# A searched table of due times, whole feature products on GpSimd, and MLP blocks of four tiles in a two-layer attention and MLP kernel

## The chip, the cores and the metric

The kernel runs on one core of one Trainium2 chip. The metric is the device time of one execution in microseconds (us). The profile's span (first to last instruction) is about 1.8 us shorter than that time, so spans are compared with spans and times with times. PE is the matmul engine, DVE the vector engine, ACT the scalar engine, POOL is GpSimd, and SP issues most DMAs.

## The reference, cut to what matters

```python
for layer in range(2):                      # the same weights in both layers
    n = layernorm(x)                        # 2048 tokens of 512, in 16 tiles of 128
    q, k, v = split(n @ wqkv)               # 32 heads of 16
    phi = lambda u: concat(softmax(u @ w_phi), softmax(-(u @ w_phi)))   # 32 features a head
    kv, z = phi(k).T @ v, phi(k).sum()      # over ALL tokens: a barrier in each layer
    x = x + (phi(q) @ kv / (phi(q) @ z + 1e-6)) @ wo
    n = layernorm(x)
    x = x + (relu(n @ W_gate) * (n @ W_up)) @ W_down        # 512 -> 1376 -> 512
```

The sum over all tokens splits each layer: first the keys of all 16 tiles, then attention and MLP tile by tile. The keys of layer 1 are made tile by tile as the MLP of layer 0 ends.

## The kernel before: the parts that matter

Each instruction group is an `Op` with an engine, an estimated cost (time the engine is held, time to the result), what it waits for, and a *due time*. A list scheduler inside the kernel, `plan`, runs all of them on paper and fixes the order on each engine. Only that order goes into the program. `port=True` marks DVE and POOL instructions which the planner keeps from overlapping on paper.

```python
for e, cand in open_.items():               # in plan(): each engine's ready operations
    ...
    t = max(clock[e], o.ready, port if o.port else 0.0, lanes[0] if o.move else 0.0)
    ...                                     # of those that can start first, the least due time wins
def refine(ops, rounds):                    # due times: plan forward, plan backward, ten times
    ...
XPOSE = (1200, 2430)                        # a DMA transpose: 1.2 us to issue, 2.43 us to land
RATE = 265.0
BLOCKS = ((1, 1, 2, 2, 2, 2, 2, 2, 2), (1, 1, 2, 2, 2, 2, 2, 2, 1, 1))   # MLP tiles per block
```

Layer 0, per tile: statistics, the scaling `xn` (DVE), a transpose (`xnTA`), K and V products (PE), two exponentials `ek` (ACT), a sum `sk` (DVE), its reciprocal (ACT), the feature product `phiK`, then the accumulating product `kvz` (PE):

```python
        n = op("DVE", SCALE, due, lambda: nc.vector.tensor_scalar(          # xn
            out=xn.t[:], in0=x_of(t), scalar1=mv[:, t, 0:1], scalar2=rs[:, t:t + 1], ...), port=True)
        ...
        a = [op("DVE", dve(512), ..., phi(nc.vector, 0, 1), ..., port=True),    # "BOTH": half on DVE
             op("POOL", (965, 975), ..., phi(nc.gpsimd, 1, 1), ..., port=True)] # half on POOL
```

In attention each tile's result `o` is transposed by DMA on SP (`oT`), and a PE projection with `wo` follows. The MLP does the same with its own input (`xnTB`). The transposes are issued one after another on SP; in the trace of the kernel before one takes 1.2 us to issue and 2.4 us to land in the median of the layers, 3.0 in the first stage.

The softmax here doesn't subtract the row's maximum and nothing guards it: scores larger than these inputs give would overflow.

## Time and profile before

| | before |
|---|---|
| time, median of the first 3 runs | 402.7 us (402.51 to 403.94) |
| span of the profiled run | 401.2 us |
| PE time by matmul count and spacing | 379.8 us |
| start of the last kvz of layer 0 | 60.4 us |
| sum of PE holes to the last matmul | 15.2 us |
| last matmul start to end of span | 3.9 us |

The third row is the number of matmuls of each width times their back-to-back spacing in the trace (216 ns for 512 columns, 109 for 256, 56 for 128). A hole is what is left between two matmul starts after that spacing.

The page of the kernel before, busy shares and the busy tenths of 40 equal slices:

```profile
PE 387.8 (97%) x3176; PEld 265.9 (66%) x3176; DVE 275.5 (69%) x685; ACT 259.5 (65%) x704; POOL 22.1 (6%) x24
...
PE   6889999899999999999999999999999999999996
...
DVE  6999896999995835787365457799998523132222
...
POOL 0142350000000000000000002000000000000000
```

PE is almost always busy, so only its holes can be won. They lie in the first six slices (60 us) and in a few later ones. The view of stretches of the kernel before (stretch, its length, busy us of each engine with instruction counts, clock, DMA share, GB/s) shows who fills the first 60 us:

```profile
10.00:20.00 10.00, 8.38 (x52) 4.16 (x53) 10.00 (x23) 8.52 (x28) 1.93 (x2) 1.00 0.23 63
20.00:30.00 10.00, 8.40 (x84) 5.32 (x81) 9.88 (x14) 8.02 (x24) 4.86 (x5) 1.00 0.82 190
30.00:40.00 10.00, 9.28 (x57) 4.55 (x56) 9.93 (x23) 8.66 (x28) 2.23 (x2) 1.00 0.73 162
40.00:50.00 10.00, 9.72 (x57) 4.95 (x58) 8.88 (x16) 9.51 (x30) 3.06 (x4) 1.00 0.93 263
50.00:60.00 10.00, 10.00 (x84) 6.05 (x82) 9.45 (x10) 9.64 (x27) 5.96 (x6) 1.00 0.42 120
```

The third busy figure is DVE: 8.9 to 10 us of every 10. Feature products and xn scalings of the kernel before in that time (views by tile; min/median/max in ns, first and last start in us):

```profile
L466 POOL TENSOR_TENSOR phiK<-ek,sk x16: 1054/1056/1717, 16.5 to 58.9; 128x512 bf16<-128x512 bf16 x16
L466 DVE TENSOR_TENSOR phiK<-ek,sk x16: 652/692/1358, 17.9 to 58.8; 128x512 bf16<-128x512 bf16 x16
L427 DVE TENSOR_SCALAR xn<-X,mvA,rsA x15: 390/403/1097, 11.5 to 45.8; 128x512 bf16<-128x512 bf16 x15
```

This is the waits view of the kernel before from 62 us to the end, PE alone (who waited for whom: us, times, longest):

```profile
PE b L607 <- ACT Eq L522: 0.4, 2, 0.3
PE b L565 <- DVE X L569: 0.4, 1, 0.4
PE q L536 <- ACT N L543: 0.4, 1, 0.4
PE b L565 <- ACT oT L376: 0.3, 1, 0.3
PE b L446 <- DMA xnTA<-xn: 0.3, 1, 0.3
```

No wait for a DMA transpose of `oT` is in it, though 28 of the 32 projections take their input from one.

### The profile page before, as it was taken

What the parts mean: (1) busy time and instruction counts of PE and PEld (TensorE: products, weight loads), DVE (VectorE), ACT (ScalarE), POOL (GpSimd) and SP (SyncE); (2) the same over time, 40 slices, a digit from 0 to 9 for tenths busy, and PEclk for the clock granted to TensorE, in tenths of its full rate; (3) what the DMA queues carried; (4) which work ended last, traced back from release to release, by engine and by line L of the source; (5) the groups of instructions that cost most, each with busy time, mean ns of one, the idle gap of its engine ahead of it and who ended that gap; (6) DMA issues with size and microseconds to landing.
All of it is one profiled execution on the core that took longest, in us unless ns stands there. A gap on an engine that the chain in (4) does not pass through costs nothing.

```text
span 401.2 us, 8365 instructions
## 1 busy us (share of the span) xinstructions
PE 387.8 (97%) x3176; PEld 265.9 (66%) x3176; DVE 275.5 (69%) x685; ACT 259.5 (65%) x704; POOL 22.1 (6%) x24
## 2 busy tenths in 40 slices
PE   6889999899999999999999999999999999999996
PEld 3454565667787678556777845576778686785784
DVE  6999896999995835787365457799998523132222
ACT  4888999977665355838464759997846353452542
POOL 0142350000000000000000002000000000000000
PEclk9999999999999999999999999999999999999999
DMA  6287940233331013101010100025333102001000
GB/s 211 63 192 159 262 118 0 42 67 63 71 68 41 0 28 67 26 15 28 2 26 2 28 0 2 1 41 81 68 65 68 28 26 68 13 29 39 15 28 28
DMA packets 54536, 21.83 MB, mean 54 GB/s; under 512 B 45952, under 2 KB 53472, under 8 KB 54496
## 3 DMA queue, kind: packets, MB, share of 16 engines
q1 hardware_dynamic: 53424, 20.25, 22.4%
q10 hardware_dynamic: 1072, 1.05, 0.8%
q8 instruction: 25, 0.41, 0.4%
q14 instruction: 15, 0.12, 0.1%
HBM read 8.44 MB, written 2.10 MB: 26 GB/s over the span
## 4 chain that ended last, share of the span: by engine, by line
PE 76%; DVE 14%; DMA 4%; ACT 3%; issue 2%; DVEq 0%; ACTq 0%
PE b L607 35%; PE b L642 18%; PE b L452 5%; PE b L446 5%; PE b L565 4%; PE b L518 3%; PE q L481 3%; DMA xnTA<-xn 3%; DVE pr L558 2%; ACT Eq L522 1%; DVE bstA L416 1%; PE q L536 1%; DVE X L569 1%; DVE m L553 1%; DVE o L561 1%
## 5 line engine op out<-in xcount | busy, mean ns | idle before, releaser
L619 ACT ACTIVATE gu<-b 128x512 bf16<-128x512 f32 (+1 forms) x102 | 55.5, 555 | 61.0 <-PE b L607 60.1
L607 PE MATMUL b<-xnTB,wg 128*128 128x256 bf16 (+3 forms) x836 | 92.9, 256 | 0.4 <-ACT Eq L522 0.3
L607 PE MATMUL b<-xnTB,wu 128*128 128x256 bf16 (+3 forms) x836 | 92.9, 256 | 0.2 <-ACT Eq L522 0.2
L625 DVE TENSOR_TENSOR hT<-gu 128x512 bf16<-128x512 bf16 (+1 forms) x102 | 38.5, 380 | 69.2 <-ACT gu L622 69.0
L642 PE MATMUL b<-wd,hT 128*128 128x512 bf16 (+1 forms) x352 | 82.8, 379 | 0.0
L607 PEld LDWEIGHTS <-wg 128*128 128x128 bf16 (+1 forms) x836 | 72.5, 100 | 11.4 <-issue 0.6
L607 PEld LDWEIGHTS <-wu 128*128 128x128 bf16 (+1 forms) x836 | 72.4, 100 | 8.1 <-issue 0.3
L622 ACT CAST gu<-b 128x512 bf16<-128x512 f32 (+1 forms) x102 | 54.8, 543 | 24.7 <-PE b L607 23.4
L642 PEld LDWEIGHTS <-hT 128*128 128x128 bf16 (+1 forms) x352 | 33.8, 98 | 34.8
L543 ACT CAST N<-q 128x384 bf16<-128x384 f32 (+1 forms) x96 | 48.1, 583 | 0.0
L522 ACT ACTIVATE Eq<-b 128x512 bf16<-128x512 f32 x64 | 40.4, 690 | 5.7 <-PE b L518 5.7
L457 DVE TENSOR_REDUCE sk<-ek 128x64 f32<-128x1024 bf16 x32 | 38.6, 1211 | 6.8 <-ACT ek L449 6.7
L648 DVE SCALAR_TENSOR_TENSOR X<-b,rsB,X 128x512 bf16<-128x512 f32 x32 | 23.3, 745 | 27.5 <-PE b L642 27.4
L449 ACT ACTIVATE ek<-b 128x512 bf16<-128x512 f32 x64 | 35.7, 603 | 8.9 <-PE b L446 8.6
L446 PE MATMUL b<-Wk,xnTA 128*128 128x512 bf16 x128 | 32.3, 380 | 4.2 <-DMA xnTA<-xn 2.1
L466 POOL TENSOR_TENSOR phiK<-ek,sk 128x512 bf16<-128x512 bf16 x18 | 21.4, 1193 | 226.6 <-ACT sk L462 221.9
L565 PE MATMUL b<-wo,oT 128*128 128x512 bf16 x128 | 32.5, 379 | 1.1 <-DVE X L569 0.4
L466 DVE TENSOR_TENSOR phiK<-ek,sk 128x512 bf16<-128x512 bf16 (+1 forms) x32 | 31.2, 977 | 2.4 <-ACT sk L462 2.3
L452 PE MATMUL b<-wv,xnTA 128*128 128x512 bf16 x128 | 32.2, 379 | 0.0
L518 PE MATMUL b<-xnTA,Wq 128*128 128x512 bf16 x128 | 31.7, 379 | 0.0
L543 ACT COPY DS<-q 128x48 f32<-128x48 f32 (+1 forms) x96 | 23.7, 318 | 7.2 <-PE q L536 6.1
L536 PE MATMUL q<-R,Eq 128*128 128x144 bf16 x256 | 25.1, 226 | 0.5 <-ACT N L543 0.4
(65 smaller groups left out, 376.1 us busy)
## 6 DMA issues: line engine op xcount, KB each, us to landing
out_dram<-X SPq DMA_DIRECT2D x16, 128.0 KB, 1.7
X<-in_A_x_dram SPq DMA_DIRECT2D x6, 256.0 KB, 4.0
wg<-in_B_W_gate_dram SPq DMA_DIRECT2D x4, 344.0 KB, 3.8
wu<-in_B_W_up_dram SPq DMA_DIRECT2D x4, 344.0 KB, 3.8
wd<-in_B_W_down_dram SPq DMA_DIRECT2D x5, 256.0 KB, 3.1
wk<-in_A_wqkv_dram ACTq DMA_DIRECT2D x2, 256.0 KB, 3.6
X<-in_A_x_dram SPq DMA_DIRECT2D x4, 128.0 KB, 4.4
wv<-in_A_wqkv_dram ACTq DMA_DIRECT2D x1, 512.0 KB, 5.4
```

Source lines behind the costliest of these rows:

```text
L446: k = op("PE", mm(4, 512), due, lambda: [nc.tensor.matmul(kp.t[:], lhsT=xnTA[c][:, b, cols], rhs=Wk2[:, b, :], start=(b == 0), stop=(b == ...
L452: v = op("PE", mm(4, 512), due_v, lambda: [nc.tensor.matmul(vp.t[:], lhsT=xnTA[c][:, b, cols], rhs=wv[:, b, :], start=(b == 0), stop=(b == ...
L457: a = op("DVE", SUM16, due, lambda: nc.vector.tensor_reduce(out=sk.t[:], in_=ek.t[:].rearrange("p s (h f) -> p (s h) f", f=DH), axis=AX.X, ...
L466: e.tensor_tensor(out=ph.t[:, s:s + n].rearrange("p s (h f) -> p (s h) f", f=DH), in0=ek.t[:, s:s + n].rearrange("p s (h f) -> p (s h) f", ...
L518: q = op("PE", mm(4, 512), due(c, b), lambda b=b, qp=qp: [nc.tensor.matmul(qp.t[:], lhsT=Wq2[:, m, b * P:(b + 1) * P], rhs=xnTA[c][:, m, : ...
L522: done.append(op("ACT", act(512), due(c, b), lambda b=b, s=s, qp=qp: nc.scalar.activation(out=Eq[c][:, b, s, :], in_=qp.t[:], func=AF.Exp, ...
L543: nc.scalar.copy(out=q[:, k, 0:3] if k < 2 else q[:, :, 3], in_=ps.t[:, 0:n * GE].rearrange("p (n c j) -> p n c j", n=n, j=HB)[:, :, lo:hi])
L565: a = op("PE", mm(4, 512), due + 3, lambda: [nc.tensor.matmul(yp.t[:], lhsT=oT.t[:, b, :], rhs=wo[:, b, :], start=(b == 0), stop=(b == NB ...
L607: nc.tensor.matmul(ps.t[:m, q * W:(q + 1) * W], lhsT=w[:, b, g * P:g * P + m], rhs=xT.t[:, b, 0:W], start=(b == 0), stop=(b == NB - 1))
L619: nc.scalar.activation(out=gu.t[:m, 0, lo * W:hi * W], in_=gp.t[:m, lo * W:hi * W], func=AF.Relu)
L622: nc.scalar.copy(out=gu.t[:m, 1, lo * W:hi * W], in_=up.t[:m, lo * W:hi * W])
L642: nc.tensor.matmul(yp.t[:], lhsT=h.t[:m, f * W + i * P:f * W + (i + 1) * P], rhs=wd[:m, f, :], start=(f == 0), stop=(f == NF - 1))
```

## The change

The intent: feed the first stage faster (value weights loaded in two pieces, early tiles and query weights first, one late load between two transposes), take the feature products of layer 0 off the full DVE, use wider matmuls in the MLP (blocks of four tiles), shorten the tail (last product in two halves), and set the order by a table of due times, found by search, in place of the kernel's own refinement.

```diff
-def refine(ops, rounds):
+def arrange(ops):
+    assert len(ops) == len(DUE)
...
-        o.n = n
+        o.n, o.due = n, DUE[n]            # DUE: a table of 2080 searched numbers (cut)
...
-XPOSE = (1200, 2430)
-RATE = 265.0
+XPOSE, XPOSE_LOADS = (1200, 2430), (1200, 3500)
+RATE = 320.0
+PHI = ["POOL"] * 15 + ["BOTH"]
-BLOCKS = ((1, 1, 2, 2, 2, 2, 2, 2, 2), (1, 1, 2, 2, 2, 2, 2, 2, 1, 1))
+BLOCKS = ((1, 1, 2, 4, 4, 2, 2), (1, 1, 2, 4, 4, 2, 1, 1))
...
-    p_xB = pool("xnTB", 3, [NB, 2 * P], fifo=True)
-    p_h = pool("hT", 2, [NF * 2 * P], fifo=True)
+    p_xB = pool("xnTB", 2, [NB, 4 * P], fifo=True)
+    p_h = pool("hT", 2, [NF * 4 * P], fifo=True)      # wk, wq and their turned copy now live in hT
...
-    l_wv = [load(3, wv[:], wqkv[:, :, 2 * D:3 * D], 524288, "ACT")   (shortened)
+    l_wv = [load(0, wv[:, b:b + 2, :], ..., 262144, "ACT") for b in (0, 2)]
+    l_wq = [load(15 + b, wq[:, b, :], wqkv[:, b, 0:D], 131072) for b in range(NB)]   # was a late load
...
+            halves = ((0, 256), (256, 512)) if l == 1 and t == T - 1 else ((0, 512),)
...
-        keys.tile(t, k0, k0 + p["V0"], k0 + p["Z0"], xT[t], "BOTH")
+        keys.tile(t, k0, k0 + p["V0"], k0 + p["Z0"], xT[t], PHI[t])
```

## The prediction

> **What bounds the kernel now.** The busy table has PE at 387.8 of 401.2 us. Busy overlaps, so I summed the spacing of matmul starts in the trace: back to back, a 512-column matmul takes 216 ns, 256 columns 109, 128 columns 56; all 3176 come to about 380 us of streaming. PE idles about 15 us plus a 4 us tail. By stretch: 4.8 us (0 to 10), 1.7, 2.3, 1.2 (to 40), none to 60, 2.9 (60 to 100), 2.3 (250 to 270), else nothing. With the first weights landing at 5.0 us (chain of waits) and a tail of 3.5, a kernel without holes would take about 387 us.
>
> The early holes come from DVE: in the table of stretches it is 89 to 100% busy from 10 to 60 us, and the chain there alternates between DVE groups and transposes. Two transposes take 4.13 us against a median of 2.5[...] (DMA share 0.7 to 0.9 there).
>
> **What the change does.**
> 1. Keys of layer 0: the whole feature product goes to POOL for 15 of 16 tiles. DVE loses 15 halves of 789 ns, 12 us of its 54. POOL gets 15 x 2 x 1.05 us (uncontended half, timeline), 32 us, up to 36 at the mean of 1.19. [...]an xn scaling of 0.40 us takes 1.10 under a POOL product. POOL becomes a serial chain from about 18 to 55-57 us. The last kvz, now at 60.4, should come 3 us earlier.
> 2. Loads: early x tiles and query weights first, one late load instead of two between transposes. The instruction order shows key weights still issued before value weights, so "value weights first" does little, and the query fold now precedes the first K. I expect the first 12 us no better, transposes near 3 us, and 1.2 us of holes gone beyond item 1.
> 3. Blocks of four: 88 gate and up matmuls of 512 columns replace 176 of 256 in each of four blocks (216 against 2 x 109 ns): 0.8 us in all.
> 4. Last product in halves: the final add (0.75 us) halves, the store (128 KB, 1.7 us) shrinks a little: 0.4 us.
> 5. Searched due times fill part of the 5 us of holes at the two attention starts, which ScalarE bounds (19.5 of 20 us busy from 60 to 80): 1.5 us.
>
> Sum 6.9 us, nearly all on the chain, because it is PE idle time.
>
> **Predicted:** 395.8 us, 8 in 10 between 391 and 400.5. Faster by over 2% (under 394.6) 0.40, within 2% 0.57, slower 0.03.
>
> **What would show it.** Last kvz at 56 to 58 us; DVE's 18 half products down to about 3, POOL busy 35 to 40 us in the first 60; DVE no longer full there; xn scaling above its 426 ns mean; first-stage transposes near 3 us; no PE hole above 0.3 us after 100 us outside the second attention start; 341 fewer matmuls at nearly the same streaming sum, 379 us; the end 0.4 us shorter.
>
> **What would make it wrong.** POOL and DVE locking each other out more than planned, holding the last kvz at 60 us; the query fold delaying the first K; a block of four making PE wait for four tiles of attention between 70 and 110 us; or the search having removed nearly all holes (389 to 391).

The sum: 3 + 1.2 + 0.8 + 0.4 + 1.5 = 6.9 us, which takes 402.7 to 395.8. What the trace of the kernel before shows of DVE beside POOL: the xn scaling at 28.39 us took 1.10 us instead of 0.40 while two POOL products ran from 26.68 to 29.33, and the POOL product at 35.43 us took 1.72 us instead of 1.05 while a DVE product of 0.68 us ran.

## More of the kernel before

Runs at full clock lie mostly within 1 us of their median, but in some executions the granted TensorE clock is halved for a few microseconds near the start (0.50 from 12 to 16 us in the profile of e4), which costs about 2 us (beside e1 to e4 the kernel before took 404.1 to 404.8 us in its four runs with a mean clock of 0.996, and 401.7 to 402.7 in the other seven). The profile lists the mean clock of each run.

## The result, and the profile after

The changed kernel took 404.52 us (median of 4 runs, 404.31 to 405.02); the kernel before in the same session took 403.12 us. Ratios here are the mean time of one kernel's fast runs over that of the other's of the same rounds, so not quite the ratio of the medians: 1.0035, 95% interval 1.0012 to 1.0058. Its verdict is "same" at 2%, but the sign is against the prediction, and the time lies outside the predicted range. A second session (e5 below) gave 1.0074.

| profiled runs, both at full clock | before | after | difference |
|---|---|---|---|
| span | 401.2 | 402.6 | +1.4 |
| start of the last kvz of layer 0 | 60.4 | 61.1 | +0.7 |
| from the last matmul of that kvz to the last matmul of all | 336.5 | 337.8 | +1.3 |
| last matmul start to end of span | 3.9 | 3.3 | -0.5 |
| PE time by count and spacing | 379.8 | 379.1 | -0.7 |
| PE holes, 0 to 20 us | 6.5 | 4.9 | -1.6 |
| PE holes, 20 to 40 us | 3.5 | 2.9 | -0.5 |
| PE holes, 40 to 60 us | 0.0 | 2.1 | +2.1 |
| PE holes, 60 us to the end | 5.2 | 7.9 | +2.7 |

The holes that vanish before 40 us come back between 40 and 60, and new ones appear in the layers. The page of the changed kernel:

```profile
PE 387.8 (96%) x2835; PEld 231.8 (58%) x2835; DVE 269.5 (67%) x659; ACT 260.8 (65%) x696; POOL 34.3 (9%) x24
...
PE   7998989998999999999999999999999999999996
...
DVE  6989955999999828752584476599999423442232
...
POOL 0338680000000000000000003000000000000000
```

The stretches of the changed kernel. DVE is still 86 to 97% busy from 20 to 50 us and has room only from 50 to 60; POOL works up to 8.2 us in 10:

```profile
20.00:30.00 10.00, 9.29 (x55) 4.37 (x53) 8.64 (x16) 8.21 (x25) 3.07 (x3) 1.00 0.63 168
30.00:40.00 10.00, 8.37 (x56) 4.33 (x55) 9.15 (x16) 9.35 (x31) 8.23 (x5) 1.00 0.92 219
40.00:50.00 10.00, 9.69 (x75) 5.33 (x73) 9.67 (x12) 8.02 (x24) 6.93 (x4) 1.00 0.66 173
50.00:60.00 10.00, 8.83 (x63) 4.54 (x61) 5.92 (x6) 9.01 (x25) 8.21 (x5) 1.00 0.62 182
```

The same products and scalings in the changed kernel:

```profile
L571 POOL TENSOR_TENSOR phiK<-ek,sk x16: 1512/1928/1975, 15.7 to 59.4; 128x1024 bf16<-128x1024 bf16 x15, 128x512 bf16<-128x512 bf16 x1
L571 DVE TENSOR_TENSOR phiK<-ek,sk x1: 694/694/694, 59.3 to 59.3; 128x512 bf16<-128x512 bf16 x1
L531 DVE TENSOR_SCALAR xn<-X,mvA,rsA x14: 383/406/2146, 12.5 to 47.3; 128x512 bf16<-128x512 bf16 x14
```

A whole product takes 1.93 us on POOL. The longest xn scaling rose from 1.10 to over 2 us. All 16 xn scalings of layer 0 together took 7.1 us before and 12.4 after (summed from the trace); four of them took 1.4 to 2.1 us each. How that travels is seen in the timeline of the changed kernel from 45 us (start, us, engine and line, what, in brackets the idle time before and what ended it):

```profile
45.30 3.86 POOL L571 TENSOR_TENSOR phiK<-ek,sk 128x1024 bf16<-128x1024 bf16 x2 [1.35 <-PE q L586]
45.93 3.38 DVE L531 TENSOR_SCALAR xn<-X,mvA,rsA 128x512 bf16<-128x512 bf16 x2
...
49.23 2.33 DVE L562 TENSOR_REDUCE sk<-ek 128x64 f32<-128x1024 bf16 x2
...
51.49 3.81 POOL L571 TENSOR_TENSOR phiK<-ek,sk 128x1024 bf16<-128x1024 bf16 x2 [2.33 <-ACT sk L567]
...
53.48 0.64 PE L586 MATMUL q<-vext,phiK 128*128 128x129 bf16 x8 [0.78 <-POOL phiK L571]
```

Two POOL products run from 45.30 to 49.16. The two xn scalings that meet them end at 49.31 instead of after some 0.8 us. The sums `sk` behind them on DVE start only then. POOL then has nothing to do for 2.33 us, because its next product needs such a sum, and PE waits for POOL. So here two POOL products of 1.93 us each made the two scalings end some 2.6 us late, and the late sums left POOL idle for 2.33 us. In the waits view of the first 62 us, PE's longest wait in total is now for these products; the view of the kernel before lists no such wait of PE:

```profile
PE q L586 <- POOL phiK L571: 2.7, 5, 1.0
```

In the layers the waits view of the changed kernel (62 us to the end, PE) has a new first line:

```profile
PE b L670 <- DMA oT<-o: 2.4, 3, 1.3
PE b L670 <- ACT oT L480: 0.5, 1, 0.5
PE b L713 <- ACT xnTB L480: 0.5, 1, 0.5
PE q L641 <- ACT DS L648: 0.3, 1, 0.3
```

The three waits end near 98.5, 124.4 and 297.4 us. This is the first of them in the timeline of the changed kernel, SP's transposes and the projection:

```profile
93.89 1.20 SPq L508 DMA_TRANSPOSE xnTB<-xn  x1
95.20 2.06 SPq L508 DMA_TRANSPOSE oT<-o  x1
...
98.55 0.82 PE L670 MATMUL b<-wo,oT 128*128 128x512 bf16 x3 [1.25 <-DMA oT<-o]
```

This transpose held SP for 2.06 us instead of 1.2, and its projection came 3.35 us after its issue. The kernel before has a slow one at the same point of the layer, for the same tile:

```profile
93.59 2.37 SPq L404 DMA_TRANSPOSE oT<-o  x1
...
103.41 0.81 PE L565 MATMUL b<-wo,oT 128*128 128x512 bf16 x3
```

There PE only asks for the result 9.8 us later, so the slow transpose costs nothing. Over all 28 `oT` transposes on SP, the projection starts a median of 6.15 us after the transpose's issue in the trace of before (1 of 28 under 4 us), and 3.56 us in the changed kernel (20 of 28 under 4 us). The searched order has used up that slack.

The planner says how it came to that. Run on paper, `plan` gives the kernel before 396.5 us and the changed one 391.9. The search found 4.6 us in the plan, and the chip returned 1.4 us of loss. The measured span exceeds the plan by 4.7 us before and 10.7 us after. About half of that growth lies in the first stage: the plan starts the last kvz at 57.9 us before and 55.7 after, the chip at 60.4 and 61.1. The other half lies after it. The plan keeps the `port=True` instructions of DVE and POOL apart: in it, DVE waits 1.9 us for POOL products in the first stage of the changed kernel (0.2 before). On the chip the scalings took 6.0 us more than 0.40 each (0.7 before).

### The profile page after: what moved, and what is told of

The parts are those of the page before. It is cut to its first block, busy times and chain, and to the rows that moved or that the text cites. A ratio compares the mean times of both kernels' runs of the same rounds, so it can differ in the third digit from the quotient of the medians.

```text
span 402.6 us, 7615 instructions
## 1 busy us (share of the span) xinstructions
PE 387.8 (96%) x2835; PEld 231.8 (58%) x2835; DVE 269.5 (67%) x659; ACT 260.8 (65%) x696; POOL 34.3 (9%) x24
## 3 DMA queue, kind: packets, MB, share of 16 engines
q10 hardware_dynamic: 1088, 1.05, 0.8%
## 4 chain that ended last, share of the span: by engine, by line
PE 65%; ACT 3%; DMA 3%; DVE 1%; issue 0%; DVEq 0%; ACTq 0%
PE b L713 33%; PE b L749 17%; PE b L670 4%; PE b L551 3%; PE b L557 3%; DMA oT<-o 2%; PE q L586 2%; ACT Eq L627 2%; PE b L623 2%; PE q L641 1%; ACT N L648 1%; DMA xnTA<-xn 1%; ACT DS L648 0%; DVE X L756 0%; PE b L511 0%
## 5 line engine op out<-in xcount | busy, mean ns | idle before, releaser
L713 PE MATMUL b<-xnTB,wu 128*128 128x128 bf16 (+5 forms) x660 | 89.0, 279 | 0.0
L713 PE MATMUL b<-xnTB,wg 128*128 128x128 bf16 (+4 forms) x660 | 88.0, 279 | 0.7 <-ACT xnTB L480 0.5
L731 DVE TENSOR_TENSOR hT<-gu 128x512 bf16<-128x512 bf16 (+4 forms) x98 | 38.4, 393 | 69.9 <-ACT gu L728 69.9
L725 ACT ACTIVATE gu<-b 128x512 bf16<-128x512 f32 (+3 forms) x98 | 54.2, 567 | 45.4 <-PE b L713 44.1
L749 PE MATMUL b<-wd,hT 128*128 128x512 bf16 (+2 forms) x363 | 81.7, 373 | 0.0
L728 ACT CAST gu<-b 128x512 bf16<-128x512 f32 (+3 forms) x98 | 53.6, 556 | 41.9 <-PE b L713 41.3
L713 PEld LDWEIGHTS <-wu 128*128 128x128 bf16 (+1 forms) x660 | 54.8, 100 | 23.6
L571 POOL TENSOR_TENSOR phiK<-ek,sk 128x1024 bf16<-128x1024 bf16 (+1 forms) x18 | 33.6, 1881 | 216.7 <-ACT sk L567 211.0
L756 DVE SCALAR_TENSOR_TENSOR X<-b,rsB,X 128x512 bf16<-128x512 f32 (+1 forms) x33 | 23.2, 728 | 23.5 <-PE b L749 23.5
L674 DVE TENSOR_TENSOR X<-X,b 128x512 bf16<-128x512 bf16 x32 | 21.6, 676 | 3.9 <-PE b L670 3.7
```

Source lines behind the costliest of these rows:

```text
L713: nc.tensor.matmul(ps.t[:m, q * W:(q + 1) * W], lhsT=w[:, b, g * P:g * P + m], rhs=xT.t[:, b, 0:W], start=(b == 0), stop=(b == NB - 1))
L725: nc.scalar.activation(out=gu.t[:m, 0, lo * W:hi * W], in_=gp.t[:m, lo * W:hi * W], func=AF.Relu)
L728: nc.scalar.copy(out=gu.t[:m, 1, lo * W:hi * W], in_=up.t[:m, lo * W:hi * W])
L731: nc.vector.tensor_tensor(out=h.t[:m, (f0 + lo) * W:(f0 + hi) * W], in0=gu.t[:m, 0, lo * W:hi * W], in1=gu.t[:m, 1, lo * W:hi * W], op=Alu ...
L749: nc.tensor.matmul(yp.t[:, 0:c1 - c0], lhsT=h.t[:m, f * W + i * P:f * W + (i + 1) * P], rhs=wd[:m, f, c0:c1], start=(f == 0), stop=(f == N ...
```

## The experiments

Two theories. **Lock**, my name for what the traces show (an xn scaling of 0.40 us took 1.10 us beside POOL products in the kernel before and up to 2.1 us in the changed kernel; the mechanism is not shown): long POOL products delay DVE's scalings, and cost in the first stage what they save. **Slack:** the table was searched with transposes of 2.43 us and packs PE work directly behind them, so each slower transpose becomes a hole. Rivals: the serial POOL chain alone; blocks of four bunching the transposes; the new loads; the scatter between runs.

All runs gave correct results, all counted as fast, and every verdict is "same" at 2%. "At full clock" is the median of the runs whose mean clock was 0.999 or more. The ratio counts all runs, also those with the clock dip; the kernel before at full clock took a median of 402.03 us in the session of e1 to e4, 402.41 in that of e5 to e8, 402.27 for e9 to e11 and 402.38 for e12. "Rest" is from the last kvz matmul of layer 0 to the last matmul. The last column is PE's waits for `oT` from 62 us on, from the waits views.

| run | time | at full clock (runs) | ratio to before, 95% | last kvz | rest | `oT` waits |
|---|---|---|---|---|---|---|
| changed kernel, first session | 404.52 | 404.52 (4) | 1.0035, 1.0012 to 1.0058 | 61.1 | 337.8 | 2.4 |
| e1 products in two on POOL | 402.73 | 402.73 (6) | 0.9991, 0.9959 to 1.0023 | 59.4 | 337.9 | 1.7 |
| e2 tiles 9 to 14 shared | 405.53 | 405.42 (4) | 1.0065, 1.0031 to 1.0099 | 61.9 | 338.0 | 1.0 |
| e3 before + fours | 404.58 | 404.26 (3) | 1.0034, 1.0004 to 1.0064 | 60.2 | 336.6 | 0 |
| e4 before + halves | 402.43 | 402.22 (4) | 0.9994, 0.9962 to 1.0026 | 62.4* | 336.3 | 0.2 |
| e5 changed kernel again | 405.01 | 404.96 (5) | 1.0074, 1.0051 to 1.0096 | 63.2* | 338.7 | 2.4 |
| e6 no table | 404.88 | 404.36 (3) | 1.0061, 1.0042 to 1.0081 | 62.7 | 335.2 | 0 |
| e7 no table, two parts, long plan | 399.82 | 399.39 (5) | 0.9937, 0.9920 to 0.9955 | 60.6* | 334.5 | 0 |
| e8 loads and halves only | 404.12 | 404.09 (5) | 1.0052, 1.0032 to 1.0072 | 60.4 | 339.2 | 2.3 |
| e9 no table, two parts | 401.59 | 401.59 (6) | 0.9970, 0.9953 to 0.9987 | 59.7 | 336.1 | 0 |
| e10 no table, long plan | 399.23 | 399.20 (5) | 0.9933, 0.9905 to 0.9960 | 58.9 | 334.5 | 0 |
| e11 as e7, blocks of two | 400.96 | 400.90 (5) | 0.9951, 0.9931 to 0.9971 | 60.1 | 335.3 | 0 |
| e12 as e7, new table | 400.01 | 399.50 (4) | 0.9924, 0.9893 to 0.9956 | 61.1 | 333.5 | 0 |

\* The profiled execution had the clock dip near the start (mean clock 0.992 to 0.996), so its last kvz is late by some 2 us (the changed kernel 63.2 in e5 against 61.1 at full clock).

### e1: POOL products in two instructions

```diff
-a = [op("POOL", POOL_PHI, due, lambda: phi(nc.gpsimd, 0, 2), [a], [ph], [ek, sk], name="phi", port=True)]
+a = [op("POOL", (965, 975), due, lambda s=s: phi(nc.gpsimd, s, 1), ...) for s in range(2)]
```

> The changed kernel, with each whole POOL product of layer 0 issued as two POOL instructions of half the size; order, engines and work are else the same, and the due times too. Theory L (lock): four xn scalings of the changed kernel took 1.4 to 2.0 us instead of 0.4[...], about 6 us of DVE lost. Under L no xn scaling should take over 1.2 us, the DVE time lost in xn should fall to 3 us or less, the last kvz of layer 0 should come at 59.5 to 60.3 instead of 61.1 us, and the time should fall by 0.8 to 1.6 us, to about 403.3. Rival R (the plan is merely slack-free and every small DMA or engine delay adds up, the lock is only where they show): time within 0.4 us of the changed kernel.

Measured: no xn scaling above 1.14 us; all 16 took 9.6 us instead of 12.4 (an excess of 2.5 over before instead of 5.3); last kvz at 59.4; time 402.73. In the ratios to before this is 0.9991 against 1.0035 and 1.0074 for the changed kernel, 1.8 to 3.3 us, but 4 of the 11 runs of the kernel before that ran beside e1 had the clock dip and none of e1's. Against the kernel before at full clock, e1 is 0.7 us longer, the changed kernel 1.4 (clocks of the kernel before not on record there) and 2.6 us (e5): a gain of 0.7 to 1.9 us, as expected. The views by tile of e1:

```profile
L534 DVE TENSOR_SCALAR xn<-X,mvA,rsA x14: 383/412/1142, 12.6 to 45.2; 128x512 bf16<-128x512 bf16 x14
L574 POOL TENSOR_TENSOR phiK<-ek,sk x31: 1052/1057/1503, 15.8 to 57.1; 128x512 bf16<-128x512 bf16 x31
```

The work, its engines and the planned span are unchanged, each POOL instruction is shorter, and POOL even works longer (2 x 1.06 against 1.93 us). PE's wait for POOL products falls from 2.7 to 1.2 us. The rest did not move (337.9), as it should. The lock theory passes this test and R's time fails, with one reserve: run on paper, the order is not wholly the same. On PE and ACT a few operations of tiles 11 to 15 changed places, so a small part of the gain may be theirs.

### e2: the last products shared again

```diff
-PHI = ["POOL"] * 15 + ["BOTH"]
+PHI = ["POOL"] * 9 + ["BOTH"] * 7
```

> The changed kernel, with the products of tiles 9 to 14 of layer 0 shared again by DVE and POOL (half each), as the kernel before has them, tiles 0 to 8 whole on POOL. In the changed kernel POOL runs four products back to back from 51.5 to 59.1 us and DVE is only 59% busy from 50 to 60. If the serial POOL chain is what holds the last kvz (theory P), it comes 1.5 to 3 us earlier, at 58 to 59.6 us, the PE holes on kvz from 46 to 56 us (1.9 us) vanish, and the time falls by 1.5 to 3 us, to about 402. If the lock losses before 50 us set it, and DVE has no room (rival), the last kvz stays at 60.5 or later and the time moves by less than 0.7 us.

Measured: last kvz at 61.9, time 405.53, no gain. The four back-to-back POOL products at the end are gone, and it did not help: the six DVE halves fill the room on DVE. So the serial POOL chain by itself does not set the last kvz; the rival of this run was right there, but not with its "less than 0.7 us": at full clock e2 is 0.8 to 2.0 us further from the kernel before than the changed kernel is. DVE's sums come before POOL's products in each tile, and what delays DVE delays all.

### e3 and e4: single parts on the kernel before

```diff
+BLOCKS = ((1, 1, 2, 4, 4, 2, 2), (1, 1, 2, 4, 4, 2, 1, 1))      # e3, with the pools it needs
+halves = ((0, 256), (256, 512)) if l == 1 and t == T - 1 else ((0, 512),)     # e4
```

> The kernel before, with blocks of four tiles in the middle of a layer (and the memory sharing they need), and nothing else of the change; its due times come from its own refinement. Streaming alone should give 0.8 us. Theory Q (fours bunch the transposes on one queue, so PE waits for an oT transpose near 97 and 296 us): at least 1 us of new PE holes in 85 to 130 and 285 to 300, time 403.3 or more, no gain. Rival (the holes there come from the searched order, not from fours): no new holes, time about 402.3.

> The kernel before, with the last product in two halves alone. Last matmul at the same time, the end after it 0.4 to 0.6 us shorter (3.3 instead of 3.9 us, as in the changed kernel), time 402.6. If the halves cost PE what they save, same time within 0.2.

e3: no holes on `oT` at the named places, so the theory that fours bunch the transposes fails there. Its profiled run (402.9 us) looks like the kernel before in both parts, with 2.1 us of new waits for ACT at the second attention start. The other two runs at full clock took 404.3 and 404.8, which the profile doesn't explain; e3 is inconclusive on the time. e4: 402.43 against 402.25, the expected 0.4 us is inside the interval and can't be seen in the time. The profile shows the end after the last matmul at 3.4 us instead of 3.9.

### e5 to e8: the table, the plan's times and the loads

> The changed kernel again, unaltered, on the same chip as the three next runs and as a measure of the scatter: earlier batches show runs of one kernel up to 3 us apart. Expected 404.5, with the last kvz of layer 0 between 60.5 and 62.5 us and the PE holes on oT transposes near 97, 124 and 296 us again, since they follow from the order.

> The changed kernel without the table of due times: the kernel's own old refinement sets them, all else as changed (loads, whole POOL products, fours, halves). Median time between a transpose landing and its projection in the plan: 0.8 us with the table, 2.0 without, 3.5 in the kernel before. The planner's own span is 394.7 without and 391.9 with the table. Theory T (the table packs the projections behind their transposes, and a transpose that is slower than planned becomes a PE hole): PE holes on oT after 64 us fall from 2.8 us to under 1, last kvz of layer 0 to last matmul takes 336.8 us or less instead of 337.8, and the time is no higher than the changed kernel's. Rival (the table is as good on the chip as in its plan): 2 to 3 us slower than the changed kernel.

```diff
-    order = arrange(ops)              # e6: the whole change with the kernel's own old refinement
+    order = refine(ops, ROUNDS)
```

> As the last, and in addition each whole POOL product in two instructions (as in e1), and the planner told that a transpose in the layers takes 1.3 us to issue and 4.2 us to land (it was told 1.2 and 2.43; the trace has 1.2 and 2.4, but up to 2.1 and 3.4 for the slow ones). If lock and missing slack are the two causes of the loss, this version should have no hole over 0.5 us on an oT transpose, no xn scaling above 1.2 us, last kvz near 59.5, and beat both kernels: 399 to 401.5. If it is not under 401.5, one of the two causes is not the whole story.

```diff
-XPOSE, XPOSE_LOADS = (1200, 2430), (1200, 3500)
+XPOSE, XPOSE_LOADS = (1300, 4200), (1200, 3500)      # e7 (with e1's edit) and e10, on top of e6
```

> Of the change only the order and spreading of the loads, the early query fold and the halves at the end: products shared by DVE and POOL on every tile, blocks of two as before, due times from refinement. The planner sees it level with the kernel before (396.6 against 396.5). Theory: the new loads only move holes within the first 60 us, since DVE is what is full there; time within 1 us of the kernel before, last kvz of layer 0 at 60 to 62. Rival (the loads were worth the 1.2 us I predicted, and POOL ate it): 1 to 2 us faster than before, last kvz under 59.5.

```diff
-PHI = ["POOL"] * 15 + ["BOTH"]           # e8: on top of e6 (its planner times stay), products and blocks as before
+PHI = ["BOTH"] * 16
-BLOCKS = ((1, 1, 2, 4, 4, 2, 2), (1, 1, 2, 4, 4, 2, 1, 1))
+BLOCKS = ((1, 1, 2, 2, 2, 2, 2, 2, 2), (1, 1, 2, 2, 2, 2, 2, 2, 1, 1))
```

e5 repeats the result, and the same waits for `oT` of 2.4 us.

e6 is 2.8 us longer than the changed kernel in the plan (394.7 against 391.9). On the chip it takes the same time, with the rest 2.6 us shorter (335.2 against 337.8), and no wait for `oT`. The waits view of e6 from 62 us on, PE:

```profile
PE q L549 <- ACT N L556: 2.5, 5, 0.9
PE b L621 <- ACT xnTB L388: 0.6, 1, 0.6
```

So the layers behave as the slack theory says. The first stage is no better (last kvz 62.7, xn scalings 11.8 us in all), which is why the time does not fall.

e7 gives 399.8 us, faster than both kernels, as expected if both causes are taken away; its longest xn scaling is 1.25 us, and PE has no wait for `oT`. (The expectation gives 3.4 us for slow transposes; the slowest in the layers took 4.0 us to land in the changed kernel.)

e8: the new loads alone make nothing faster; the last kvz stays at 60.4 as before. The time is 1.7 us longer, not within 1 us as expected. I had put 1.2 us of gain on the loads. And its trace has waits for `oT` like the changed kernel's, without any table:

```profile
PE b L578 <- DMA oT<-o: 2.3, 3, 1.3
```

The three transposes took 4.1 us to land; run on paper, the refined order had put their projections 2.8 to 3.4 us after the issue. So a table isn't needed for these holes. But of the six refined orders made with a transpose of 2.43 us (before, e3, e4, e6, e8, e9) only e8 has more than 0.2 us of them, while the four runs with the table all have 1.0 us or more.

### e9 and e10: the two causes apart

> e6 (no table) with each whole POOL product in two instructions, transposes planned at 2.43 us as before. With e6 (404.9), e7 (399.8) and the next run it makes a square: product whole or in two, transposes planned short or long. [...]if the two parts of e7 add up, this run and the next together give its 5.1 us. If the order alone (chance of the refinement) made e7 fast, this run stays at 404.5 or above.

Its forecast was 403 us, if products in two instructions are worth the 1.8 us that e1 showed.

> e6 (no table) with the planner told that a transpose takes 4.2 us, whole POOL products. If the long plan for transposes is worth about 3 us: 401.5 to 402.5, with the time from last kvz of layer 0 to the last matmul near e7's 334.5 us (it was 335.2 in e6, 337.8 in the changed kernel), but with xn scalings of up to 2 us in the first stage and a last kvz of 62 or later.

With e6 and e7 these make a square (medians at full clock in us; in brackets the difference to the kernel before at full clock in the same session, as e6 and e7 ran in another session than e9 and e10):

| | transposes planned at 2.43 us | planned at 4.2 us |
|---|---|---|
| product whole on POOL | e6 404.36 (+1.95) | e10 399.20 (-3.07) |
| product in two instructions | e9 401.59 (-0.68) | e7 399.39 (-3.02) |

The two parts do not add. In the short plan the two instructions are worth 2.6 us (by the brackets), but not by the shorter POOL instructions alone: the refinement runs anew in each cell, and on paper e9 is already 1.0 us shorter than e6 (393.7 against 394.7). e1, which keeps the table, found 0.7 to 1.9 us. With the long plan the order alone is worth 5.0 us, and then halving the POOL instructions gives nothing: what long ones cost depends on the order. In e10 the xn scalings are still slow (up to 1.71 us, 9.6 us in all), but the last kvz is at 58.9, where I had expected 62 or later, and PE waits only 0.2 us for POOL products in the first 62 us. The waits view of e10 from 62 us on has no DMA wait of PE at all:

```profile
PE b L621 <- ACT xnTB L388: 1.0, 2, 0.7
PE q L549 <- ACT N L556: 0.6, 2, 0.4
```

Of the 4.5 us between the profiled runs of e6 and e10, the rest gives only 0.7; 3.8 us lie before the last kvz. A long time for the layers' transposes changes the due times of the first stage too, through the backward pass, and this order happens to be good there: PE waits 1.6 us for `xnTA` transposes in e10's first 62 us and 3.5 us in e6's. That I had not aimed at, and I can't show that it would come again.

### e11 and e12: fours or twos, and a second search

> e7 with the blocks of two of the kernel before in place of fours. If fours are worth only their streaming, 0.8 us slower than e7: 400.6. If they are worth nothing because they cost filler work at the attention starts (as e3 suggests, where they gave back what they saved): within 0.3 us of e7. If they cost time: faster than e7.

> A searched table of due times again, for the same changed kernel (products in two POOL instructions of 1.06 us as measured), but searched with transposes planned at 1.3 us to issue and 4.2 us to land in the layers and 4.5 us in the first stage, where the table of the change was searched with 1.2, 2.43 and 3.5. The planner's span under those long times falls from 397.8 (order of e7) to 392.7. If a search as such spoils the order on the chip (any gain in the plan is noise): 400 or more. If the change's table failed because the times it was searched with were too short, this one gives more than half of the planned 5 us: 395.5 to 398.5, without a PE hole over 0.5 us on an oT transpose, and beats every kernel so far.

e11: with blocks of two the version takes 400.96 instead of 399.82 us (1.5 us more at full clock, in another session). The rest is 0.8 us longer, which is the streaming. Fours are worth that much once the order has slack; the other 0.7 us is within what runs of one kernel differ by.

e12 was searched with layer transposes at 1.3 and 4.2 us, those of the first stage at 1.3 and 4.5 instead of 1.2 and 3.5, and POOL halves at their measured 1.06 us. The planned 5 us did not come. 400.01 us is as fast as e7 and no faster, and misses what I expected. The rest is the shortest of all (333.5) and without `oT` waits, but the first stage ends at 61.1 where its plan said 57.1. Searching with longer transposes cured what it was meant to cure. The first stage kept the gain; that the plan has its loads, its waits between DVE and POOL and its starts too simple is my guess and is not shown.

One comparison covers all runs. Run each kernel's planner on paper and take its rest from the measured one. The chip needs 1.9 us more than planned for the kernel before; 5.2 to 6.2 us more in the four runs with the first table (the changed kernel, e1, e2, e5); 3.8 us more in e8; and 1.4 to 1.8 us more in all others, e12 with its second table among them. So neither a search (e12) nor the short transposes (e6) cost the rest by themselves; together they did in all four runs. The waits for `oT` are only their largest sign: with the same table they vary from 1.0 to 2.4 us while the rest stays at 337.8 to 338.7, and in e1 and e2 PE waits 0.7 us for an `xnTB` transpose instead.

## Why the prediction was wrong, point by point

Items 1 and 2 were to bring the last kvz 4.2 us earlier; it came 0.7 us later. Items 3 and 5 were to shorten the rest by 2.3 us; it grew by 1.3. The end went as predicted. These two misses, 4.9 and 3.6 us, are the whole error.

- **What bounds the kernel** held: PE streaming 379.8 us, little to win, only holes.
- **Item 1 failed.** The step was "POOL becomes a serial chain from about 18 to 55-57 us. The last kvz ... should come 3 us earlier." It came 0.7 us later. I had one scaling of 1.10 us beside POOL products in hand, but sized it as a detail. The step left out what the POOL chain does to DVE: with products of 1.93 us the scalings lost 5.3 us, the delay went round through the sums to POOL itself (2.33 us idle at 49 to 51 us), and PE waited 2.7 us for POOL products. The DVE products went from 16 to 1 and DVE had room after 50 us, as predicted; POOL was busy 30 us in the first 60, not 35 to 40. e1 shows it for this order: with shorter POOL instructions the last kvz came 1.7 us earlier (but for the few operations that changed places). e2 shows that the POOL chain was not the bound I took it for, and e10 that another order can carry whole products without the loss.
- **Item 2 failed in its size.** I expected 1.2 us from the loads. Holes in the first 40 us did fall by 2.1 us (1.6 of them in the first 20, where I expected nothing), but the stage did not end earlier; e8, with the loads without the POOL products, ends it at the same 60.4 us as before. Transposes of the first stage landed in a median of 2.9 us, near the 3 predicted, but before it was 3.0 as well.
- **Item 3 held**: the streaming fell by 0.7 us (0.8 predicted), and 341 fewer matmuls ran.
- **Item 4 held**: the end is 0.5 us shorter (0.4 predicted), in the profiles; e4's time can't show so little.
- **Item 5 failed, with the wrong sign.** "Searched due times fill part of the 5 us of holes ...: 1.5 us." Holes after 60 us grew by 2.7 us; the waits view puts 2.4 us on PE's waits for `oT`, which it does not list before. I took a search for free, and did not compare planned slack. The instruction order was at hand before the run, and with it how soon each projection follows its transpose. e6 removes the table: waits gone, rest 2.6 us shorter. e12 keeps a search but with longer transposes: waits gone too, rest 4.2 us shorter. What failed is the search together with the transpose time that it was given.
- What could make it wrong: I named POOL and DVE delaying each other, "holding the last kvz at 60 us", and that came. The query fold did not delay the first K much (10.8 us against 10.2). Fours making PE wait for four tiles was not what happened.

What stays open: why single transposes take 2 us to issue instead of 1.2; why e3's timed runs are slower than its profiled one; how much of e1's gain is the shorter POOL instructions alone; and which feature of e10's first stage is worth the 3.8 us.

## What to carry to other kernels

An order searched in a cost model uses up every slack that the model thinks free; search it with the slow end of what the trace shows for each wait (here 4.2 instead of 2.43 us for a transpose: the four runs planned with it have no `oT` wait of PE), or compare the time from each DMA's issue to its use before and after. When work is moved to GpSimd, ask how long one of its instructions lasts and look in the trace for DVE instructions that get longer beside it (here scalings of 0.40 us took up to 2.1 us beside products of 1.93 us); two short instructions can beat one long one (e1), or make no difference (e7 against e10). Judge the parts of a change under a robust order: the same structure that lost 0.35% with its table won 0.67% (e10) with the refinement and transposes planned at 4.2 us, while the refinement with 2.43 us lost 0.61% (e6).

## What the traces show of the hardware here

- DVE beside POOL: bf16 scalings of 0.40 us took up to 2.1 us beside POOL products of 1.93 us, and up to 1.14 us beside products of 1.06 us (e1). The sums of bf16 to f32 kept their 1.2 us beside a POOL product (three of 1.22 us in the changed kernel from 51.9 to 58.2 us, while POOL worked from 51.5 to 59.1). Splitting the GpSimd instruction shortened the loss here, for 0.18 us more POOL work per product.
- The clock dip comes only in some runs: in 8 of 44 runs of the kernel before in the four later sessions the mean clock was 0.996 or less and the time 403.8 to 405.8 us, against 401.7 to 403.5. The stretches of e5's profile show such a dip, with a clock of 0.64 from 8 to 10 us and 0.51 from 10 to 12 (the figure after the POOL column is the clock):

```profile
6.00:8.00 2.00, 1.39 (x20) 1.05 (x20) 1.07 (x4) 1.81 (x5) 0.00 (x0) 1.00 1.03 329
8.00:10.00 2.00, 1.34 (x13) 1.34 (x14) 1.83 (x5) 0.77 (x3) 0.00 (x0) 0.64 0.89 301
10.00:12.00 2.00, 2.00 (x22) 2.00 (x20) 1.80 (x5) 1.53 (x4) 0.00 (x0) 0.51 0.25 86
```

  No run here shows what starts the dip.
- A transpose by DMA (128 x 512, bf16) took 2.4 us in the median to landing in the layers and up to 4.0 us in the changed kernel and 4.3 in the kernel before, up to 5.0 us in the first stage of the changed kernel, and had an issue of 1.2 us that was 1.6 to 2.4 us in a few.
